# AV with stationary probabilities and a column of ones in V, rows scaled before a DMA transpose, in a chunk-attention and MLP kernel

## The chip, the cores and the metric

The kernel runs on one core of one Trainium2 chip. Its time is device microseconds of one execution. Engines that matter here: TensorE (PE, with its weight loads shown as PEld), VectorE (DVE), ScalarE (ACT), GpSimd (POOL) and SyncE (SP), which does no arithmetic and issues nearly all DMAs, in program order. The DMAs themselves run on 16 DMA engines that all queues share.

## The reference

Attention over chunks of 64 positions, 8 batches of 8 heads with 576 positions and 64 features, then an MLP with an exact GELU on the 4608 rows of 512 features:

```
scores = q_c @ k_c^T / sqrt(64)            # per head, per chunk of 64
attn   = exp(scores - max) / (sum + 1e-9)
x      = (attn @ v_c), heads side by side   # 4608 x 512
out    = gelu(x @ w_in) @ w_out             # 512 -> 2048 -> 512, f32 in, f32 out
```

The kernel works in bf16 with f32 sums, and leaves out the maximum (the scores are small).

## The kernel before

**Tiles.** The 4608 rows are nine tiles of 512 (`NT = 9`): tile t below 8 holds the first 512 positions of batch t, tile 8 the last 64 positions of all batches. A pass of the loop at L1003 does the MLP of tile t and, in the gaps, the attention of tile n = t+1. The result of the attention is `x`, kept transposed (features on partitions, `[128, 4, 512]`), because both operands of the first product need the contraction on partitions.

**The MLP of a tile.** `mm1_groups` (L582) does x @ w_in. It uses a seven-product scheme instead of eight block products for three of the four column groups (a, b, c) and plain products ("p") for the rest; the order is a string of words such as "begin 1a c1a p 6a 1b ...", read from left to right. The words 1 to 7 are the products, c and a are copies and additions on ACT and DVE, g the GELUs. Products 4 to 7 need sums of blocks of x, `x_sums` (L548, four DVE subtractions T1, T3, T2, T4). From tile 3 (`FIRST7`) on the second product is `mm2_seven` (L681), also seven products: X, Y(s2), X, Y(s1), Z(s3), Y(s4), Z, with hooks `also(0)` to `also(5)` between them. Tiles 0 to 2 use plain products in 16 slots of four matmuls (`mm2_slot`, L765).

**The attention of tile n.** `quad_S` (L224) does 64 small matmuls (64x64 blocks in the four quadrants of the array) into four PSUM banks, and four ACT exponentials make the probabilities `pT`, keys on partitions, queries along the free axis. Then, before the change:

- `quad_part` (L246), four times: a DVE transpose in 32x32 blocks and a DVE reduction give partial sums over keys.
- `quad_exchange` (L258) and `quad_across` (L271): small copies between partition groups, on ACT up to tile 3 and on POOL after it (`small`, L278).
- `quad_rb` (L264): totals and their reciprocals, DVE.
- `quad_rc` (L291), four times: a DVE transpose spreads the reciprocals along the partitions.
- `quad_av` (L296): 64 small matmuls with V stationary and `pT` moving; the result comes out transposed already.
- `quad_x` (L304), four times: a DVE multiplication of the PSUM result by the spread reciprocals writes `x`.

**Where these stand.** In pass 1 and 2 (`one_tile`, L990): S at slot 1, the partial sums at once, totals at slot 3, AV and `quad_x` and `x_sums` at slot 7; in pass 2 the S of tile 4 at slot 14. From pass 3 on: AV at `also(1)`, `x_sums` at `also(2)` and `also(3)`, the next S at `also(2)`, partial sums at `also(3)` to `also(5)`, and exchange, totals and the first spread in the words of the next `mm1_groups` (`totals_over_mm1`, L972; in pass 3 the words pt0 to pt3, ex0, ex1 of `FOURTH`).

**Loads.** All go through SP in program order: k and q of tile t+3, v of tile t+2 (`load_v_rows`, nine DMAs), 1 MB each, then the transposes of q and k by DMA (`flip`, L187, 16 blocks of 128x128 each, after POOL has cast them to bf16 at L160), and the stores of the output rows. Pass 3 and later issue them as `ahead` (L1027): flips of t+2, v of t+2, q and k of t+3. At most eight DMAs of SP are under way; a ninth waits for the first.

**PSUM.** Eight banks: `ps_mm` 3, `ps_tp` 2, `ps_at` 3. AV and S use two of `ps_tp` and two of `ps_at`.

Of the kernel before, what the change touches and what calls it, by code (L numbers as in the profile page):

```python
# [11 lines left out]
def kernel(  # L12
# [134 lines left out]
    def cast_v_plain(t, copy, ns=range(CT // 2)):  # L147
        st = tiles[t]
        if 0 in ns:
            st["v"] = ld.tile([P, H, CT // 2, D], bf16, tag="v", name="v_nat")  # L150
        for n in ns:
            copy(st["v"][:, :, n], st["vf"][:, :, n])
# [51 lines left out]
    def cast_v_rows(t, copy):  # L204
        st = tiles[t]
        st["v"] = ld.tile([P, H, CT // 2, D], bf16, tag="v", name="v_nat")
        for r in range(2):
            copy(st["v"][:, r::2], st["vf"][:, r::2])  # L208
# [32 lines left out]
    def quad_parts(t):  # L241
        for g2 in range(2):
            for c in range(2):
                quad_part(t, g2, c)

    def quad_part(t, g2, c):  # L246

        st = tiles[t]
        if c == 0:
            st["part", g2] = work.tile([P, 2, NB // 2, 2, 2], f32, tag="part", name="part", bufs=2)  # L250
        pt = work.tile([P, NB // 2, 32, 2], bf16, tag="pt", name="pt", bufs=2)
        nc.vector.transpose(
            pt[:].rearrange("p n e u -> p (n e u)").bitcast(f32).rearrange("p (n e) -> p n e", e=32),
            st["pT", 2 * g2 + c][:].rearrange("p i c -> p (i c)").bitcast(f32).rearrange("p (n e) -> p n e", e=32))
        nc.vector.tensor_reduce(st["part", g2][:, c, :, :, 0], pt[:].rearrange("p n e u -> p n u e"),  # L255
                                axis=mybir.AxisListType.X, op=mybir.AluOpType.add)

    def quad_exchange(t, g2):  # L258
        part = tiles[t]["part", g2]
        for s in range(G):  # L260
            o = s ^ 1
            small(t)(part[QD * s:QD * (s + 1), :, :, :, 1], part[QD * o:QD * (o + 1), :, :, :, 0])

    def quad_rb(t, g2):  # L264
        total, rb = (work.tile([P, 2, NB], f32, tag=nm, name=nm, bufs=2) for nm in ("total", "rb"))
        nc.vector.tensor_reduce(total[:], tiles[t]["part", g2][:].rearrange("p c n u s -> p c (n u) s"),
                                axis=mybir.AxisListType.X, op=mybir.AluOpType.add)
        nc.vector.reciprocal(rb[:], total[:])
        tiles[t]["rb0", g2] = rb

    def quad_across(t, g2):  # L271
        rb = tiles[t]["rb0", g2]
        across = work.tile([P, NB], f32, tag="across", name="across", bufs=2)
        tiles[t]["rb", g2] = rb[:, 0], across[:]
        for r in range(2):
            small(t)(across[CH * r:CH * (r + 1)], rb[CH * (1 - r):CH * (2 - r), 1])

    def small(t):  # L278
        return AC if t <= FIRST7 else PO

    def quad_total(t):
        for g2 in range(2):
            quad_exchange(t, g2)
        for g2 in range(2):
            quad_rb(t, g2)
            if g2 == 0:
                tiles[t]["rb", 0] = tiles[t]["rb0", 0][:, 0], None
                quad_rc(t, 0, 0)
            quad_across(t, g2)

    def quad_rc(t, g2, c):  # L291
        rc = work.tile([P, NB, 32], f32, tag="rc", name="rc", bufs=4)
        nc.vector.transpose(rc[:], tiles[t]["rb", g2][c].to_broadcast([P, NB, 32]))
        tiles[t]["rc", 2 * g2 + c] = rc

    def quad_av(t):  # L296
        st = tiles[t]
        st["av"] = four_banks("av_ps")
        for g2, u, g, n, r, c, o, rs, os in quadrants():
            nc.tensor.matmul(st["av"][g2][c][rs, u, :], st["v"][os, 2 * g + r, place(r, 2 * n + c)[1], :],  # L300
                             st["pT", 2 * g2 + c][os, u, :],
                             start=True, stop=True, tile_position=(CH * o, CH * r))

    def quad_x(t, g2, c):  # L304
        st = tiles[t]
        x = st["x"][:].rearrange("p g (n c e) -> p (g n) c e", c=2, e=CH)[:, CT * g2:CT * (g2 + 1), c]
        nc.vector.tensor_tensor(x.rearrange("p n (e u) -> p n e u", u=2),  # L307
                                st["av"][g2][c][:].rearrange("p n (e u) -> p n e u", u=2),
                                st["rc", 2 * g2 + c][:].rearrange("p (n u) e -> p n e u", u=2),
                                op=mybir.AluOpType.mult)  # L310
# [47 lines left out]
    def duo_av(t, g2):  # L358
        st = tiles[t]
        st.setdefault("av", {})[g2] = duo_banks(g2, "av_ps")  # L360
        for u, g, n, r, c, rs, cs in duos(g2):
            nc.tensor.matmul(st["av"][g2][c][rs, u, :], st["v"][cs, 2 * g + r, n, :], st["pT", 2 * g2 + r][cs, u, :],
                             start=True, stop=True, tile_position=(CH * c, CH * r))
# [39 lines left out]
    def att_rc(t, g):  # L403

        rb = tiles[t]["rb"]
        rc = work.tile([P, NB, 32], f32, tag="rc", name="rc", bufs=4)
        nc.vector.transpose(rc[:], rb[:, g].to_broadcast([P, NB, 32]))
        tiles[t]["rc", g] = rc
# [25 lines left out]
    def att_av(t, g2, ns):  # L434
# [5 lines left out]
        for g in (2 * g2, 2 * g2 + 1):  # L440
            for n, r, c, i, rs, cs in parity_blocks(ns):
                nc.tensor.matmul(st["av", g2][c][rs, g % 2, n], st["v"][cs, 2 * g + r, n, :], st["pT", g][cs, r, n],
                                 start=True, stop=True, tile_position=(CH * c, CH * r))
# [104 lines left out]
    def x_sums(t, which=(1, 3, 2, 4)):  # L548
# [7 lines left out]
        for i in which:  # L556
# [13 lines left out]
               g12c w2 w4 g21c"""  # L570

    FOURTH = """begin pt2 tab 1a 1b pt0 c1a c1b p 7a 6a 2a 2b 6b c2a pt3 5a g11a c3a c2b 1c 5b a1a c1c g11b 3a g22a
                pt1 6c c3b 4a 7b ex0 c2c a2a g12a ex1 2c g11c g21a p 3b a1b totals 4b a2b g12b 5c 7c c3c g22b a1c
                g21b p 3c 4c g22c h1 a2c g12c g21c rc0 h2 p h3"""
# [106 lines left out]
    def mm2_seven(t, at={}):  # L681
# [9 lines left out]
        X, Y, Z = (ps_mm.tile([P, 2, NH], f32, tag="mm", name="y_ps") for _ in range(3))  # L691
# [3 lines left out]
        if t == B:  # L695
            s1 = work.tile([P, 2, NH], f32, tag="y_1", name="y_1", bufs=1)
            last_seven(t, h, w, s, T, (X, Y, Z), (s1, s2, s5), y)
# [3 lines left out]
        AC(Y[:], X[:])  # L701
        h_third(t)
        also(1)
# [61 lines left out]
    def mm2_slot(t, ms, qt):  # L765
        st = tiles[t]
        if qt == 0:
# [101 lines left out]
    with tc.manual_schedule():  # L869
# [102 lines left out]
        def totals_over_mm1(n):  # L972

            at = ("begin", "totals", "rc0")
            units = [[lambda: quad_exchange(n, 0), lambda: quad_exchange(n, 1)],
                     [lambda: quad_rb(n, 0), lambda: quad_rb(n, 1), lambda: quad_across(n, 0),
                      lambda: quad_across(n, 1)],
                     [lambda: quad_rc(n, 0, 0)]]
            return dict(zip(at, units))
        def loads_at(t, nms="qk"):  # L980
            if t + 2 < NT:
                load_v_rows(t + 2)
            if t + 3 < NT:
                for nm in nms:
                    load_qk(t + 3, nm)
# [4 lines left out]
        def one_tile(n, more={}):  # L990

            at = {0: [lambda: act_table(Act.Exp)], 1: [lambda: quad_S(n), lambda: quad_parts(n)],
                  3: [lambda: quad_total(n)],
                  7: [lambda: quad_av(n), lambda: quad_x(n, 0, 0)]
                     + [u for m in range(1, G)
                        for u in (lambda m=m: quad_rc(n, m // 2, m % 2), lambda m=m: quad_x(n, m // 2, m % 2))]
                     + [lambda: x_sums(n)]}
# [5 lines left out]
        for t in range(1, NT):  # L1003
# [4 lines left out]
            if t == 1:  # L1008
# [5 lines left out]
                e1 = {"1a": [lambda: w_in_sums(slice(0, 2), "c")], "p": [lambda: load_v_rows(3)], "end": [lambda: w_sums((1, 3))]}  # L1014
                e2 = one_tile(2, {5: [lambda: act_table(Act.Gelu)],
                                  8: [lambda: flips_of(3), lambda: loads_of_qk(4)]})
            elif t == 2:
# [3 lines left out]
                e1.update({f"w{i}": [lambda i=i: w_sums((i,))] for i in (2, 4)})  # L1021
                flips_of(4)
                loads_at(2, "q")
                cast_v_rows(4, PO)
                e2 = one_tile(3, {8: [lambda: load_qk(5, "k")], 14: [lambda: quad_S(4)]})
            elif n < NT:
                def ahead(t=t):  # L1027
                    if t + 2 < NT:
                        flips_of(t + 2)
                    loads_at(t)  # L1030
                e1 = totals_over_mm1(n)
                if t == FIRST7:
                    pool_cast_q(t + 2)
                    del e1["begin"]
                    e1["tab"] = [lambda: act_table(Act.Gelu)]
                    e1.update({f"ex{i}": [lambda i=i: quad_exchange(n, i)] for i in range(2)})
                    e1["totals"] += [lambda: pool_cast_k(FIRST7 + 2), ahead]
                    e1.update({f"pt{i}": [lambda i=i: quad_part(n, i // 2, i % 2)] for i in range(G)})
                else:
                    if t + 2 < NT:  # L1040
# [45 lines left out]
```

## Time and profile before

| | us |
|---|---|
| runs | 273.24, 275.71, 277.56 (median 275.71) |
| profiled execution | 274.82 |
| its span | 273.0 |
| outside the span | 1.8 |
| PE busy | 260.3 (95%) |
| DVE busy | 220.4 (81%) |
| ACT busy | 181.8 (67%) |
| POOL busy | 91.2 (33%) |

The span is the time from the first to the last instruction of the program; the granted TensorE clock was 1.0. Groups of instructions are given as line, engine, operation, output<-input, shape, and a count, then busy us and the mean ns of one. Where two instructions of an engine follow each other without a pause, the next starts a little before the first ends, so that sums of means are up to a tenth too high. "SPq" rows are the issuing time on SP, not the transfer; the time from issue to landing is a separate figure. The passes are seen in the trace by the first X product of each: pass 2 begins at 80.75, pass 3 at 109.50, pass 4 at 136.99, pass 5 at 163.92, pass 6 at 190.84, pass 7 at about 217.6, pass 8 at about 243.5 us.

Landing times, from issue to landing (median): q loads of 1 MB 6.2 us, k loads of 256 KB 6.2 us, v loads of 128 KB 3.0 us, stores of 256 KB 3.3 us, transposes of q 4.9 us and of k 3.8 us.

### The profile page before, as it was taken

Reading aid. Unit: us, or ns where it says so; the run is one execution under the profiler, and the core shown is the slowest. Engines: PE = TensorE matmul, PEld = TensorE weight load, DVE = VectorE, ACT = ScalarE, POOL = GpSimd, SP = SyncE. Lnnn points to the kernel's source line nnn. Section 1 sums busy time; section 2 is a strip of 40 time slices with the busy share of each in tenths; the row PEclk is TensorE's granted clock in tenths of the full one; section 3 lists DMA queues with packets and bytes.
Section 4 is the critical chain, followed back from the end, with each engine's and each line's share of the span. In section 5 each row is a group of like instructions: output and inputs, shape, how many; then the busy total and the mean of one; then the engine's idle time right before and its main releaser. Section 6 shows DMA issues by size and latency. Waiting matters only on the chain.

```text
span 273.0 us, 7454 instructions
## 1 busy us (share of the span) xinstructions
PE 260.3 (95%) x2984; PEld 187.3 (69%) x3009; DVE 220.4 (81%) x386; ACT 181.8 (67%) x353; POOL 91.2 (33%) x180
## 2 busy tenths in 40 slices
PE   8689999999999999999999999999999999999993
PEld 2454454486448644768887888788878887888782
DVE  2663586979796999999989998999899889945852
ACT  3557755788667966986679567946884787338700
POOL 2725667360460443370372355133510321000000
PEclk9999999999999999999999999999999999999999
DMA  6999999996999998999899796987983410130005
GB/s 202 258 359 405 396 394 246 242 268 151 347 222 241 279 176 181 273 231 188 231 265 248 219 249 93 237 192 155 251 121 86 143 41 2 38 111 7 4 0 154
DMA packets 118066, 53.96 MB, mean 198 GB/s; under 512 B 93456, under 2 KB 112912, under 8 KB 118032
## 3 DMA queue, kind: packets, MB, share of 16 engines
q1 hardware_dynamic: 117712, 52.97, 74.8%
q8 instruction: 23, 0.38, 0.6%
q10 hardware_dynamic: 320, 0.52, 0.5%
q14 instruction: 11, 0.09, 0.1%
HBM read 36.70 MB, written 9.44 MB: 169 GB/s over the span
## 4 chain that ended last, share of the span: by engine, by line
PE 80%; DVE 7%; SPq 4%; ACT 3%; DMA 3%; issue 1%; POOL 0%; ACTq 0%; DVEq 0%
PE y_ps L673 27%; PE h_Y L611 11%; PE h_ps L631 8%; PE h_Z L611 8%; PE h_X L611 8%; PE y_ps L771 6%; PE h_ps L481 5%; PE y_ps L795 4%; DMA arrival<-in_moe_w_in_dram 3%; SPq L145 2%; PE s_ps L230 1%; SPq L112 1%; DVE part L255 1%; DVE x L368 1%; ACT y_ps L701 1%
## 5 line engine op out<-in xcount | busy, mean ns | idle before, releaser
L611 PEld LDWEIGHTS <-w_in_s 128*128 128x128 bf16 x384 | 37.4, 98 | 6.8
L673 PEld LDWEIGHTS <-h_s 128*128 128x128 bf16 x384 | 37.0, 98 | 5.4 <-DVE h_s L513 0.8
L673 PE MATMUL y_ps<-w_t,h_s 128*128 128x256 bf16 x288 | 34.7, 273 | 0.3
L611 PEld LDWEIGHTS <-w_in_sb 128*128 128x128 bf16 x288 | 28.1, 98 | 8.3 <-issue 2.0
L208 POOL CAST v_nat<-arrival 128x1024 bf16<-128x1024 f32 x14 | 15.4, 1106 | 53.3 <-DMA arrival<-in_v_dram 46.7
L160 POOL CAST q_nat<-arrival 128x512 bf16<-128x512 f32 x33 | 22.2, 711 | 32.5 <-DMA arrival<-in_q_dram 24.2
L771 PE MATMUL y_ps<-w_out_sb,h 128*128 128x512 bf16 x137 | 31.5, 379 | 1.3 <-issue 1.0
L673 PEld LDWEIGHTS <-h 128*128 128x128 bf16 x288 | 28.2, 98 | 4.7
L631 PE MATMUL h_ps<-x,w_in_sb 128*128 128x512 bf16 x103 | 27.8, 379 | 0.7
L611 PE MATMUL h_Y<-x_t,w_in_s 128*128 128x256 bf16 x192 | 27.6, 272 | 0.0
L611 PE MATMUL h_X<-x,w_in_sb 128*128 128x256 bf16 x192 | 26.8, 273 | 0.0
L655 DVE TENSOR_TENSOR y<-h_Z,y 128x512 f32<-128x512 f32 x32 | 21.6, 680 | 5.8 <-PE h_Z L611 4.9
L160 POOL CAST k_nat<-arrival 128x512 bf16<-128x512 f32 x34 | 22.1, 684 | 11.6 <-DMA arrival<-in_k_dram 7.6
L771 PEld LDWEIGHTS <-h 128*128 128x128 bf16 x144 | 13.4, 98 | 15.6 <-issue 0.8
L673 PE MATMUL y_ps<-w_out_sb,h 128*128 128x256 bf16 x192 | 22.9, 273 | 0.0
L618 ACT ACTIVATE h<-y 128x512 bf16<-128x512 f32 x32 | 20.1, 628 | 1.7 <-DVE y L655 1.6
L867 ACT ACT_TABLE_LOAD x16 | 20.5, 1283 | 1.0 <-PEq L1070 0.7
L644 ACT COPY h_Y<-h_X 128x512 f32<-128x512 f32 x24 | 14.0, 584 | 10.5 <-PE h_X L611 10.4
L255 DVE TENSOR_REDUCE part<-pt 128x16 f32<-128x512 bf16 x28 | 19.2, 686 | 1.0
L633 ACT ACTIVATE h<-h_ps 128x512 bf16<-128x512 f32 x29 | 17.1, 595 | 2.6 <-PE h_ps L631 1.2
L307 DVE TENSOR_TENSOR x<-av_ps,rc 128x512 bf16<-128x512 f32 x28 | 18.0, 670 | 0.6
L631 PEld LDWEIGHTS <-w_in_sb 128*128 128x128 bf16 x116 | 11.4, 98 | 7.7
(129 smaller groups left out, 488.7 us busy)
## 6 DMA issues: line engine op xcount, KB each, us to landing
out_dram<-y_sb SPq DMA_DIRECT2D x32, 256.0 KB, 3.3
arrival<-in_q_dram SPq DMA_DIRECT2D x7, 1024.0 KB, 6.2
arrival<-in_k_dram SPq DMA_DIRECT2D x24, 256.0 KB, 6.2
arrival<-in_v_dram SPq DMA_DIRECT2D x42, 128.0 KB, 3.0
arrival<-in_moe_w_out_dram SPq DMA_DIRECT2D x4, 1024.0 KB, 12.4
arrival<-in_v_dram SPq DMA_DIRECT2D x8, 256.0 KB, 8.3
arrival<-in_moe_w_in_dram SPq DMA_DIRECT2D x4, 512.0 KB, 7.3
arrival<-in_moe_w_in_dram SPq DMA_DIRECT2D x2, 1024.0 KB, 10.4
```

The lines of the kernel that those rows point to most:

```text
L160: copy(st[nm][:, g].rearrange("p j r d -> p r j d"), st[nm + "f"][:, 2 * g:2 * g + 2])
L208: copy(st["v"][:, r::2], st["vf"][:, r::2])
L255: nc.vector.tensor_reduce(st["part", g2][:, c, :, :, 0], pt[:].rearrange("p n e u -> p n u e"), axis=mybir.AxisListType.X, op=mybir.AluOpT ...
L307: nc.vector.tensor_tensor(x.rearrange("p n (e u) -> p n e u", u=2), st["av"][g2][c][:].rearrange("p n (e u) -> p n e u", u=2), st["rc", 2 ...
L611: nc.tensor.matmul(banks[g + name][:, i], lhs[:, kk, i], rhs[:, kk], start=fresh and i == kk == 0, stop=(kk == 1), skip_group_check=True)
L618: nc.scalar.activation(h[:, j:j + 2, m], src[:], Act.Gelu)
L631: nc.tensor.matmul(bank[:], w_in_sb[:, ks, f * P:(f + 1) * P], st["x"][:, ks, :], start=(ks == 0), stop=(ks == KS - 1))
L633: nc.scalar.activation(st["h"][:, f, :], bank[:], Act.Gelu)
L655: TT(sums[g, i][:], banks[g + "Z"][:], sums[g, i][:], op=add)
L673: nc.tensor.matmul(out[m], lhs[:, f, m * P:(m + 1) * P], rhs[:, f, :], start=fresh and f == 0 and (m == 0 or len(out) == 3), stop=(f == FH ...
L771: nc.tensor.matmul(y_ps[:], st["h"][:, f, ms * P:(ms + 1) * P], w_out_sb[:, f, :], start=(f == 0), stop=(f == FF - 1))
L867: nc.scalar.activation(act_scratch[:], rest[:, 0:1], func)
```

## The change

- V gets a 65th column (`D + 1`), set to ones by a small POOL memset from tile 2 on (`FIRSTX = 2`; "the third tile").
- `quad_part`, `quad_exchange`, `quad_rb`, `quad_across`, `quad_total`, `quad_rc` and `quad_x` are gone. `rows_av` has `pT` stationary and V moving: 64 matmuls with 65 columns each, into six banks of seven (or two) blocks of 65: two of `ps_tp`, three of `ps_at`, one of `ps_mm`. Queries now lie on partitions, and column 64 is the sum of each row.
- `rows_x` takes, bank by bank, a reciprocal of the sums and a multiplication into `x_r` (bf16, SBUF), and transposes `x_r` into `x` with two DMAs on SP, 7 blocks after the second bank, 9 after the sixth.
- The `ps_mm` bank is that of the fourth row block (pass 1 and 2) or the Z bank of `mm2_seven`, whose allocation moves behind the first copy; `h_third` moves behind `also(1)`.
- AV stands at slot 6 instead of 7 and `x_sums` at slot 14 (pass 1 and 2), or at `also(4)`. Two of the `w_sums` (2 and 4) move from pass 2 to pass 1, behind `rows_x`.
- Loads: v of tile 3 and 4 move behind the transposes of x of passes 1 and 2; in pass 3 and later `ahead` issues v of t+2, the flips and q of t+3, and `behind` at `also(2)` issues k of t+3 (and v of tile 8). In pass 3 the flips come before v.

```diff
+            nc.gpsimd.memset(st["v"][:, :, :, D:], 1.0)
...
+    def rows_av(t, last):
+        banks = [pool.tile([P, MT], f32, tag=tag, name="av_ps")
+                 for pool, tag in ((ps_tp, "tp"),) * 2 + ((ps_at, "at"),) * 3] + [last]
+        st["av"] = [b[:, :NX * (D + 1)].rearrange("p (i e) -> p i e", e=D + 1) for b in banks]
+        for b in range(G * CT // 2):
             for c in range(2):
...
+                for r in range(2):
+                    bank, i = 2 * (b // NX) + r, b % NX
+                    g, n, o = b // (CT // 2), b % (CT // 2), c ^ r
+                    os, cs = slice(CH * o, CH * (o + 1)), slice(CH * c, CH * (c + 1))
+                    nc.tensor.matmul(st["av"][bank][cs, i, :],
+                                     st["pT", 2 * (g // 2) + c][os, CT // 2 * (g % 2) + n, :],
+                                     st["v"][os, 2 * g + r, place(r, 2 * n + c)[1], :],
+                                     start=True, stop=True, tile_position=(CH * o, CH * c))
+    def rows_x(t):
+        rows = work.tile([P, G * CT // 2, 2, D], bf16, tag="x_r", name="x_r", bufs=1)
+        xT = st["x"][:].rearrange("p g (n e) -> p (g n) e", e=P)
+        def flip_rows(b0, b1):
+            nc.sync.dma_start_transpose(xT[:, b0:b1], rows[:, b0:b1].rearrange("p b r d -> p (b r d)"))
+        for bank in range(6):
+            b0 = NX * (bank // 2)
+            ni = min(NX, G * CT // 2 - b0)
+            av = st["av"][bank][:, :ni]
+            one = work.tile([P, NX], f32, tag="one", name="one", bufs=2)
+            nc.vector.reciprocal(one[:, :ni], av[:, :, D])
+            to = rows[:, b0:b0 + ni, bank % 2]
+            nc.vector.tensor_tensor(to, av[:, :, :D], one[:, :ni].to_broadcast([P, ni, D]), op=mybir.AluOpType.mult)
+            if bank == 1:
+                flip_rows(0, NX)
+        flip_rows(NX, G * CT // 2)
...
-                  3: [lambda: quad_total(n)],
-                  7: [lambda: quad_av(n), lambda: quad_x(n, 0, 0)]
...
+            at = {0: [lambda: act_table(Act.Exp)], 1: [lambda: quad_S(n)],
+                  6: [lambda: rows_av(n, bank_of_rows()), lambda: rows_x(n)], 14: [lambda: x_sums(n)]}
...
+                                  6: [lambda: w_sums((2, 4))], 7: [lambda: load_v_rows(3)], 8: [lambda: flips_of(3), lambda: loads_of_qk(4)]})
...
+                load_qk(5, "q")
+                e2 = one_tile(3, {7: [lambda: load_qk(5, "k")], 8: [lambda: load_v_rows(4)], 14: [lambda: quad_S(4)]})
...
                 def ahead(t=t):
+                    if t > FIRST7 and t + 2 < B:
+                        load_v_rows(t + 2)
                     if t + 2 < NT:
                         flips_of(t + 2)
-                    loads_at(t)
+                    if t == FIRST7:
+                        load_v_rows(t + 2)
+                    load_ahead(t, "q")
+
+                def behind(t=t):
+                    if t + 2 == B:
+                        load_v_rows(B)
+                    load_ahead(t, "k")
...
+                    e1["begin"] = [lambda: pool_cast_qk(5), lambda: cast_v_rows(4, PO), ahead]
...
+                e2 = {1: [lambda: rows_av(n, tiles[n - 1]["Z"]), lambda: rows_x(n)], 2: [behind], 3: [], 4: [lambda: x_sums(n)]}
```

More of the change, by code (lines that the diff above doesn't have):

```diff
@@ L258, in quad_exchange @@
[L258 to L310, printed above, removed]
+    NX = MT // (D + 1)
@@ L405, in att_rc @@
         rb = tiles[t]["rb"]
[L406 removed]
+        rc = work.tile([P, NB, 32], f32, tag="rc", name="rc", bufs=2)
         nc.vector.transpose(rc[:], rb[:, g].to_broadcast([P, NB, 32]))
@@ L690, in mm2_seven, with bank_mm @@
         T = [None] + [w_t[i] for i in range(1, 5)]
-        X, Y, Z = (ps_mm.tile([P, 2, NH], f32, tag="mm", name="y_ps") for _ in range(3))
+        def bank_mm():
+            return ps_mm.tile([P, 2, NH], f32, tag="mm", name="y_ps")
+        X, Y = bank_mm(), bank_mm()
         s2, s5 = (work.tile([P, 2, NH], f32, tag=nm, name=nm, bufs=1) for nm in ("y_2", "y_5"))
@@ L766, in mm2_slot @@
         st = tiles[t]
-        if qt == 0:
+        if qt == 0 and ("y_ps", ms) not in st:
             st["y_ps", ms] = ps_mm.tile([P, d_model], f32, tag="mm", name="y_ps")
@@ L1037 @@
[L1037 to L1040, printed above, removed]
-                        e1["begin"] += [lambda: pool_cast_k(t + 2)]
-                    e1["begin"] += [ahead]
-                e2 = {1: [lambda: quad_av(n), lambda: quad_rc(n, 0, 1), lambda: quad_x(n, 0, 0), lambda: quad_x(n, 0, 1),
-                          lambda: quad_rc(n, 1, 0), lambda: quad_rc(n, 1, 1),
-                          lambda: quad_x(n, 1, 0), lambda: quad_x(n, 1, 1)],
-                      2: [lambda: x_sums(n, (1, 3))], 3: [lambda: x_sums(n, (2, 4))]}
+                e2 = {1: [lambda: rows_av(n, tiles[n - 1]["Z"]), lambda: rows_x(n)], 2: [behind], 3: [], 4: [lambda: x_sums(n)]}
```

81 lines of the change are left out of this document (27 added, 54 removed).

## The prediction

> **What bounds the kernel.** I read the page's busy shares and chain first.
>
> ```profile
> PE 260.3 (95%) x2984; PEld 187.3 (69%) x3009; DVE 220.4 (81%) x386; ACT 181.8 (67%) x353; POOL 91.2 (33%) x180
> ...
> DMA  6999999996999998999899796987983410130005
> ...
> PE 80%; DVE 7%; SPq 4%; ACT 3%; DMA 3%; issue 1%; POOL 0%; ACTq 0%; DVEq 0%
> ```
>
> PE carries the chain, and the DMA engines are full until slice 31 (some 210 us). Next the stretches by pass (length; busy PE, PEld, DVE, ACT, POOL; clock, DMA share, GB/s):
>
> ```profile
> 53.33:80.75 27.42, 26.76 (x285) 16.66 (x288) 23.01 (x41) 20.57 (x45) 10.97 (x16) 1.00 0.93 246
> 80.75:109.50 28.75, 28.17 (x353) 17.60 (x357) 25.67 (x44) 21.58 (x47) 9.38 (x11) 1.00 1.02 220
> 109.50:136.99 27.49, 27.16 (x342) 21.79 (x341) 26.81 (x48) 21.27 (x38) 9.82 (x23) 1.00 0.96 230
> 136.99:163.92 26.93, 26.78 (x340) 21.82 (x341) 25.45 (x44) 19.55 (x35) 12.75 (x26) 1.00 0.96 245
> 163.92:190.84 26.92, 26.77 (x340) 21.89 (x341) 25.04 (x44) 19.55 (x35) 9.88 (x22) 1.00 0.85 169
> ```
>
> PE idles 0.66, 0.58, 0.33, 0.15 and 0.15 us in them, and 0.15 each in passes 6 and 7: 2.2 us in all. The rest of its 12.7 idle us lies before 53 and in the last pass, which the change does not touch. DVE is nearly as full, but what it ends late costs PE at most those 2.2 us.
>
> **What is removed and added**, by shape:
>
> ```profile
> L255 DVE TENSOR_REDUCE part<-pt 128x16 f32<-128x512 bf16 x28 | 19.2, 686 | 1.0
> L307 DVE TENSOR_TENSOR x<-av_ps,rc 128x512 bf16<-128x512 f32 x28 | 18.0, 670 | 0.6
> L252 DVE STREAM_TRANSPOSE pt<-pT 128x256 f32<-128x256 f32 x28 | 12.2, 436 | 2.0 <-ACT pT L237 2.0
> ...
> L450 DVE TENSOR_TENSOR x<-av_ps,rcs 128x256 bf16<-128x256 f32 x4 | 1.5, 420 | 0.9 <-PE av_ps L442 0.9
> ...
> L421 DVE RECIPROCAL rr<-sT 128x8 f32<-128x8 f32 x2 | 0.4, 208 | 0.8 <-PE sT L416 0.8
> ```
>
> DVE loses per tile four each of these transposes, reductions and multiplications (0.436 + 0.686 + 0.670), four spreads (0.697), two totals (0.190), two reciprocals (0.353): 11.0 us. It gains six reciprocals (0.208, L421) and six multiplications; 670 ns for 512 and 420 for 256 elements make 0.98 ns an element, so 0.607 for 448 and 0.294 for 128: 1.25 + 2.43 + 0.59 = 4.3 us. Seven tiles save 47 us of DVE, 5.1 of ACT (16 x 219 + 8 x 202 ns), 12.2 of POOL (40 x 209 + 20 x 193 ns; seven memsets of about 0.13 come in, L63). All of it lies beside PE: worth 0 to 2.2 us, and I take 1.0, nearest to passes 1 and 3, whose DVE queues it empties. POOL's casts of V now write runs of 65: 1.1 us (L208) to double that, under POOL's two thirds idle.
>
> AV stays 64 small matmuls. It takes 0.67 us in the chain, and so does S, which visits the quadrants in another order; in the trace four start within 12 ns and the next four 32 ns later. A 65th column adds 27/64 ns to each group of four: nothing. If the new order of quadrants ran them one by one, 64 x 27 ns (a quarter of the 109 ns pitch of a 256-column matmul) would be 1.75 us, 7.5 in seven tiles. I take nothing, the row of S and AV being nearer.
>
> **A pass from the fourth on.** T0 is the end of AV (152.23 in pass 4); the next pass starts at T0+11.5, and its first product that needs `x_sums` (6a, third of four subtractions, 1.8 us) at T0+12.8. So the second transpose has to land by T0+10.9. DVE ends its h sums at 152.99, T0+0.8; bank 2 is done at T0+2.4, bank 6 at T0+5.0. Sixteen blocks land 3.8 (k) to 4.9 us (q) after issue, so nine land by T0+9.9 at the full price: hidden with 1 us to spare, 3 at half of it. `h_third` now follows the six banks: 5.0 + 1.22 gives T0+6.2, just when Z needs it (158.41, T0+6.2): 0 to 0.1 us a pass, 0.5 in five; I take 0.2.
>
> **SP, where the transposes have to pass.** What stands ahead of them in pass 2 and 3:
>
> ```profile
> 94.41 2.15 SPq L193 DMA_TRANSPOSE q_t<-q_nat  x1
> 98.80 1.61 SPq L193 DMA_TRANSPOSE k_t<-k_nat  x1
> 100.46 5.30 SPq L126 DMA_DIRECT2D arrival<-in_v_dram  x9
> 105.80 0.60 SPq L112 DMA_DIRECT2D arrival<-in_q_dram  x1
> 106.50 1.00 SPq L787 DMA_DIRECT2D out_dram<-y_sb  x2
> 107.55 8.45 SPq L106 DMA_DIRECT2D arrival<-in_k_dram  x4
> ...
> 124.78 5.98 SPq L126 DMA_DIRECT2D arrival<-in_v_dram  x9
> 130.80 0.60 SPq L112 DMA_DIRECT2D arrival<-in_q_dram  x1
> ```
>
> SP never rests here, and a transfer waits for those ahead: the store issued at 67.23, behind two loads of 1 MB, landed after 8.1 us, not 3.3; the q load of 130.80 landed at 136.62. A pair of q and k transposes between two landings took 3.9 us (144.38 to 148.17), so the 16 blocks of x cost 2.0 to 2.4 of this full stream.
>
> Pass 1: AV at slot 6 ends at 71.7, bank 6 at 75.5; the loads ahead have landed by 75.4, so x lands at 78.8, 1.5 us before pass 2 needs it. v of tile 3 follows only then: SP is 3 us later at the flips of tile 3 (k_u lands at 87.9; DVE reaches `in_order` at 89.3, covering it by 1.4), and k of tile 4 lands at 97.0, not 95.4.
>
> Pass 2: POOL casts k of tile 4 (3.34 us) before SP can go on, so its flip goes out at 100.4 and lands at about 104.1, 2.9 before S at 107.0 needs it; q of tile 5 at 102.0, landing at 108.2 (4.2 us of stream, as 132.43 to 136.62); a store; then x of tile 3, ready on DVE since 103.5, lands at 111.2. Pass 3 would start at 109.2 and needs T3 for 7a, its fourth step: 112.5 instead of 111.2. Late by 1.3 us (0 to 3).
>
> Pass 3: x of tile 4 stands behind k and v of tile 4/5, both flips, v and q of tile 6. From k of tile 4 (95.4) to q of tile 6 (136.6) the same set took 41.2 us before, 3.7 of them gaps. Now it starts at 97.0 and has x of tile 3 in it (2.2): 97.0 + 41.2 + 2.2 = 140.4, or 136.7 without the gaps. x lands 2.2 later, 138.9 to 142.6, and T2 1.85 after that; 6a ran at 138.14 before. Late by 2.6 to 6.3, the delay of pass 2 included; DVE, which stands in `x_sums` meanwhile, holds back a store and the next copies, and these hold nothing else. I take 4.0, near the middle: pass 3 showed gaps before (POOL's copies of L262 and L276) that are gone, and has no new ones but for the casts of tile 5. v of tile 4 (cast by 122.4) is still 3 us before its AV; past that each us would be paid.
>
> Pass 4 and later: v, flips, q, k, x and stores need about 23.5 us of stream in 26.9, so the lag melts and the first reckoning holds.
>
> Sum: 274.8 (the profiled execution, 0.9 below the median) - 1.0 + 0.2 + 4.0 = 278.0; with one half of the 0.9 added, since the runs scatter from 273.2 to 277.6, **278.5 us**.
>
> **Rivals.** The bound of 2% is 5.5 us, about what a measurement of this kernel can tell from no change: 269.3 and 280.3 around 274.8.
>
> - *The full stream decides more* (chance 0.23): the gaps stay and each x pair costs what q_t cost at 117.48 (3.98 us of issue). Two of these in place of 2.2 add 3.5 to 142.6, and a half of it less: late by 8 to 10, 282 to 284. For it: SP's 3.98; against: k_t's 1.6 to 2.2. From a lag of 5.5 us on it is over the bound.
> - *Nothing is held* (0.18): SP reaches x in time, and it lands after 3.8 to 4.9 us everywhere. Then PE's 2.2 idle us are all that is left: 272.6 to 274.8, say 273.9. Against it: the store of 67.23.
> - *AV one quadrant after another* (0.03): 278 + 7.5, 285.5.
> - *A gain over 2%* (0.03): only if PE's own matmuls ran closer together; no idle time in the passes supports it.
> - *Each block pays by itself* (0.01): nine blocks have 5.9 us (T0+5.0 to T0+10.9), so it decides from 0.65 us a block on; at twice that the 16 blocks run 20.8 us from bank 2, to T0+23.2, 12.3 late in seven passes: 361. Against it: 16 blocks land in 3.8 to 4.9, 0.24 to 0.31 each.
>
> The Trainium skill (VectorE: DVE Perf Modes, "The three transpose paths") prices a 128x128 bf16 transpose by DMA at 1309 ns and by TensorE at 390, which is that last rival and speaks against this change. The trace disagrees for many blocks in one DMA (0.24 us each at best), and the measurement decides.
>
> The forecast has the remaining 0.52; its own range is 277.0 to 280.8 (late by 2.6 to 6.3), of which I put 0.04 over the bound. So faster 0.03; within 2% 0.48 + 0.18 = 0.66; slower 0.04 + 0.23 + 0.03 + 0.01 = 0.31. The range, 273.5 to 283.5, leaves out the gain (0.03), the two dear rivals (0.04), the top of the stream's case (0.06) and the bottom of the unheld one (0.05).
>
> **What would show it.** Right: DVE about 175 us busy, PE unchanged in busy time, S and AV at 0.67; PE idle 1 to 2 us at the start of pass 3 and 2 to 5 at that of pass 4, released by DVE's `x_sums` or the transposes of x, which wait on SP behind the q loads; none in passes 5 to 8. Wrong: x landing under 5 us after bank 6 in pass 3; PE waiting in every pass (then on `h_third` or the Z bank); AV above 1 us.

## The result and the profile after

| | before | after |
|---|---|---|
| runs, us | 273.24 to 277.56 (4), median 275.5 | 283.48 to 287.22 (4), median 285.25 |
| profiled execution (span) | 274.82 (273.0) | 284.48 (282.7) |
| PE busy | 260.3 | 265.5 |
| DVE busy | 220.4 | 173.0 |

The changed kernel is slower: the ratio is 1.038, with an interval from 1.027 to 1.049. Said were 278.5 us and a range up to 283.5; the time lies above the range. The page of the changed kernel first (busy us and share; then the granted clock and the DMA engines in 40 slices; then the chain's shares):

```profile
PE 265.5 (94%) x3009; PEld 188.8 (67%) x3009; DVE 173.0 (61%) x330; ACT 176.9 (63%) x329; POOL 78.8 (28%) x127
...
PEclk9599999999999999999979999999999999999998
DMA  7999998997989999998999979999943642151004
...
PE 69%; DVE 12%; DMA 11%; SPq 3%; ACT 2%; issue 2%; POOL 1%; DVEq 0%; ACTq 0%; POOLq 0%
```

DVE lost 47 us, as reckoned, and the chain grew longer all the same: DMA's share in it went from 3% to 11%. In slice 21 the clock digit is 7: PE ran at half clock for part of it, which no slice of the kernel before shows. (The 5 in slice 2 lies in the first 15 us, before the passes that the change touches; the last section comes back to it.) The stretches by pass (columns as in the prediction):

```profile
53.89:81.08 27.19, 27.17 (x286) 16.64 (x286) 22.40 (x38) 18.16 (x33) 10.40 (x16) 1.00 0.94 240
81.08:111.73 30.65, 29.23 (x357) 17.63 (x356) 13.19 (x26) 18.94 (x35) 8.93 (x13) 1.00 1.11 239
111.73:141.71 29.98, 27.29 (x341) 21.75 (x341) 17.51 (x35) 21.19 (x37) 8.96 (x14) 1.00 0.94 222
141.71:171.88 30.17, 28.57 (x340) 22.44 (x341) 19.44 (x39) 19.82 (x35) 10.33 (x14) 0.94 1.00 230
171.88:198.80 26.92, 26.90 (x345) 22.12 (x343) 17.64 (x36) 19.56 (x35) 6.85 (x11) 1.00 1.01 211
```

Against 28.75, 27.49, 26.93 and 26.92 before, pass 2 is 1.9 us longer, pass 3 2.5, pass 4 3.2, pass 5 not at all; 0.3 were lost ahead of pass 2 and 1.7 behind pass 5. That is the whole 9.7 us. PE's gaps in them, from the trace: 1.25 us in pass 2 (93.00 to 94.25, waiting for DVE, which waits at `in_order` for k_u); 0.17 + 1.24 at the start of pass 3 and 1.37 + 1.58 at that of pass 4, all released by the transposes of x; and 1.66 in pass 7 (233.85 to 235.51), released by ACT's copy `h_sb` of group c. The longest waits of PE (who waited for what; us in total, times, longest), and then that copy of ACT, which had itself waited for a store:

```profile
PE h_ps L602 <- DMA x<-x_r: 2.8, 2, 1.6
PE h_Y L582 <- ACT h_sb L623: 1.7, 1, 1.7
PE h_X L582 <- DMA x<-x_r: 1.5, 2, 1.4
PE h_Z L582 <- DVE h_sb L626: 1.3, 1, 1.3
```

```profile
234.87 0.58 ACT L623 COPY h_sb<-h_Y 128x512 f32<-128x512 f32 x1 [2.20 <-DMA out_dram<-y_sb]
```

In pass 4 there is one thing more: from 144.38 on the clock is at half for 3.41 us, in which eight matmuls of 256 columns took 1.85 us (at 146.14) and the next eight at full clock 1.04, so about 1.7 us, half of it, are lost with PE busy (28.57 against 26.78).

This is where x waits, on SP (start, issuing time, operation):

```profile
103.30 0.57 SPq L112 DMA_DIRECT2D arrival<-in_q_dram  x1
103.97 0.53 SPq L762 DMA_DIRECT2D out_dram<-y_sb  x1
104.59 6.03 SPq L270 DMA_TRANSPOSE x<-x_r  x2
...
134.76 0.61 SPq L112 DMA_DIRECT2D arrival<-in_q_dram  x1
135.47 5.01 SPq L270 DMA_TRANSPOSE x<-x_r  x2
```

A pair of transposes behind a q load of 1 MB holds SP for 5 to 6 us; in passes 4 to 7 one transpose takes 1.2 to 1.6. The second of each pair landed 7.19 us (114.19) and 6.89 us (144.07) after its issue.

### The profile page after: what moved, and what is told of

It reads as the page before. It is cut to its first block, busy times and chain, and to the rows that moved or that the text cites. A ratio compares the mean times of both kernels' runs of the same rounds, so it can differ in the third digit from the quotient of the medians.

```text
span 282.7 us, 7352 instructions
## 1 busy us (share of the span) xinstructions
PE 265.5 (94%) x3009; PEld 188.8 (67%) x3009; DVE 173.0 (61%) x330; ACT 176.9 (63%) x329; POOL 78.8 (28%) x127
## 4 chain that ended last, share of the span: by engine, by line
PE 69%; DVE 12%; DMA 11%; SPq 3%; ACT 2%; issue 2%; POOL 1%; DVEq 0%; ACTq 0%; POOLq 0%
PE y_ps L644 22%; PE h_Y L582 9%; PE h_Z L582 7%; PE h_X L582 6%; PE h_ps L602 6%; DMA x<-x_r 5%; PE h_ps L452 4%; PE y_ps L746 4%; PE y_ps L770 4%; DVE x_r L278 2%; DVE h_s L484 2%; DMA k_u<-k_nat 2%; DMA arrival<-in_k_dram 2%; DVE h_s L483 2%; SPq L126 2%
## 5 line engine op out<-in xcount | busy, mean ns | idle before, releaser
L602 PE MATMUL h_ps<-x,w_in_sb 128*128 128x512 bf16 x116 | 30.3, 383 | 2.8 <-DMA x<-x_r 2.8
L746 PE MATMUL y_ps<-w_out_sb,h 128*128 128x512 bf16 x144 | 32.8, 380 | 0.0
L160 POOL CAST k_nat<-arrival 128x512 bf16<-128x512 f32 x34 | 20.6, 642 | 33.9 <-DMA arrival<-in_k_dram 24.8
L582 PE MATMUL h_X<-x,w_in_sb 128*128 128x256 bf16 x192 | 27.7, 279 | 1.5 <-DMA x<-x_r 1.5
L623 DVE COPY y<-h_Y 128x512 f32<-128x512 f32 x16 | 11.0, 686 | 20.8 <-PE h_Y L582 19.4
L278 DVE TENSOR_TENSOR x_r<-av_ps,one 128x448 bf16<-128x448 f32 (+1 forms) x35 | 19.5, 558 | 1.2
```

Of the source, the lines that this page charges most:

```text
L160: copy(st[nm][:, g].rearrange("p j r d -> p r j d"), st[nm + "f"][:, 2 * g:2 * g + 2])
L278: nc.vector.tensor_tensor(to, av[:, :, :D], one[:, :ni].to_broadcast([P, ni, D]), op=mybir.AluOpType.mult)
L582: nc.tensor.matmul(banks[g + name][:, i], lhs[:, kk, i], rhs[:, kk], start=fresh and i == kk == 0, stop=(kk == 1), skip_group_check=True)
L602: nc.tensor.matmul(bank[:], w_in_sb[:, ks, f * P:(f + 1) * P], st["x"][:, ks, :], start=(ks == 0), stop=(ks == KS - 1))
L746: nc.tensor.matmul(y_ps[:], st["h"][:, f, ms * P:(ms + 1) * P], w_out_sb[:, f, :], start=(f == 0), stop=(f == FF - 1))
```

## Experiments

The theory after the result: AV, DVE and the new chain cost nothing; the loss is the transposes of x standing on SP among loads, and it is paid wherever the next reader of the late queue is: x itself, k_u, the stores. The clock adds to it. Each kernel was timed together with the kernel before on the same chip (median 274.2 to 275.0 there).

**1. Without the transposes of x.** `rows_x` writes its rows straight into x.

```diff
-        rows = work.tile([P, G * CT // 2, 2, D], bf16, tag="x_r", ...)
+        rows = st["x"][:].rearrange("p g (n r d) -> p (g n) r d", r=2, d=D)
-                flip_rows(0, NX)
-        flip_rows(NX, G * CT // 2)
```

> The transposes of x by DMA are left out: the rows go untransposed into x, so the output is not the reference's; all loads, the six banks, the scaling on DVE and the moved sums stay. Theory (the loss is x landing late behind loads on SP, and the clock at half after the stalls): the gaps of PE at the starts of pass 3 and 4 (0.17 + 1.24 + 1.37 + 1.58 us) are gone, the granted clock stays at 1.0 from pass 2 to 7 (1.7 us back), and the gap before in_order's product (1.25) shrinks, since SP reaches the flips of tile 3 some 3 us sooner; the gap of 1.66 us in pass 7 stays. About 277.5 to 279 us, a ratio of 1.01 to the kernel before. Rival (the 65-column AV, the new DVE chain or the order of the loads cost it): 283 to 286, no different from the changed kernel. Rival (the clock falls whatever PE waits for): a half-clock period between 100 and 270 us in spite of the missing gaps.

274.99 us, a ratio of 1.001 (0.997 to 1.004): less than the theory had given. Busy times and granted clock of its page:

```profile
PE 260.7 (96%) x3009; PEld 187.2 (69%) x3009; DVE 173.3 (64%) x330; ACT 176.4 (65%) x329; POOL 80.3 (30%) x127
...
PEclk9999999999999999999999999999999999999999
```

No gap over 0.2 us is left in passes 2 to 4, the gap of pass 7 is 0.17 instead of 1.66, and the clock stays at full. So all of the loss hangs on the transposes, the one in pass 7 too. The same run says what the rest of the change is worth together, DVE's relief of 47 us among it: nothing that can be measured.

**2. The transposes issued, and nobody waits for them.** As in 1, but the two DMAs are issued, from x into a dead buffer.

```diff
+        rows = st["x"][:].rearrange("p g (n r d) -> p (g n) r d", r=2, d=D)
+        xT = work.tile([P, G * CT // 2, P], bf16, tag="x_r", name="x_dead", bufs=1)
```

> The rows go untransposed into x, as in the run without transposes (so the output is not the reference's), but the two transposes of x are issued all the same, from x into a buffer that nobody reads. So SP and the stream carry them, and nothing waits for their landing. Theory (two parts: x itself late, about 6 us with the clock; and what the transposes push back on SP, about 3 us): the gaps at the starts of pass 3 and 4 and the half clock are gone, those in pass 2 (some 1.2) and pass 7 (some 1.6) stay: 275.0 + 2.9 = 278. Rival (only the wait for x costs): 275 to 276, no gap in passes 2 and 7. Rival (it is the load on the stream itself, through other loads that land late): 281 or more.

285.43 us (1.039, 1.031 to 1.047), as slow as the changed kernel; this is over what the theory gave, and its rival of 281 or more has the time. The gaps that the theory left in passes 2 and 7 are there (1.30 and 1.75 us). But there is a third, which it did not have, and what PE waits for there is not a load: it stands from 145.72 to 151.03, 5.31 us, for one copy of ACT. SP and ACT there:

```profile
133.47 0.61 SPq L112 DMA_DIRECT2D arrival<-in_q_dram  x1
134.18 5.89 SPq L270 DMA_TRANSPOSE x_dead<-x  x2
140.16 0.53 SPq L737 DMA_DIRECT2D out_dram<-y_sb  x1
140.75 4.17 SPq L106 DMA_DIRECT2D arrival<-in_k_dram  x4
145.02 2.22 SPq L737 DMA_DIRECT2D out_dram<-y_sb  x3
```

```profile
150.39 0.59 ACT L623 COPY h_sb<-h_Y 128x512 f32<-128x512 f32 x1 [5.86 <-DMA arrival<-in_v_dram]
```

`h_sb` of group c takes a buffer of the output rows (`ypool`, two of them), so it may be written when the stores of pass 3 have left it. These stand on SP behind the dead transposes and four k loads, and the one that empties the first of the two buffers lands at 150.24, 0.15 ahead of the copy. The label names a load of v, but none landed between 135.6 and 151.0, and the semaphore that ACT waited for until then is that of this store, issued at 146.25. Without anyone waiting for x, PE runs ahead into the same hole in SP's queue, 5 us later. Two windows of half clock follow (148.09 to 154.92). So the held queue costs PE time also where nobody waits for x; in the changed kernel x was only the first of its readers.

**3. q behind x.** The q loads of tiles 5 and 6 are moved behind the transposes of x.

```diff
-                load_qk(5, "q")
-                e2 = one_tile(3, {7: [lambda: load_qk(5, "k")], ...
+                e2 = one_tile(3, {7: [lambda: loads_of_qk(5)], ...
...
-                    load_ahead(t, "q")
+                    if t > FIRST7:
+                        load_ahead(t, "q")
...
+                    if t == FIRST7:
+                        load_ahead(t, "q")
                     load_ahead(t, "k")
+                    if t == FIRST7:
+                        pool_cast_q(t + 3)
...
```

> The changed kernel with the q loads of tiles 5 and 6 moved behind the transposes of x (in pass 2 into slot 7 with k; in pass 3 to also(2), with POOL's cast of it). Theory: x of tile 3 and 4 land 3.5 to 4.5 us sooner, the time of one load of 1 MB on the full stream: before 110.5 and before 140.5, so the gaps at the starts of pass 3 and 4 are gone and with them the half clock: 4.4 + 1.7 us less, about 279 us. Rival (the two transposes take 7 us under any load, for the reads of the stream that are still there): gaps of 1 us and more stay at both places, 283 or more.

279.52 us (1.018, 1.010 to 1.025), 5.7 us less, of 6.1 expected. x of tile 3 lands at 104.45 and 106.66, 3.0 and 3.3 us after issue; x of tile 4 at 134.68 and 136.02. The load ahead was the price, and the half clock is gone with the gaps. 0.68 us of gap is left at `in_order`, and the stores of pass 3 now stand behind five loads, so that the copy `h_sb` is late in pass 4: a new gap of 2.12 us (145.05 to 147.17), and 1.04 in pass 7.

**4. v of tile 8 first.** The 16 loads that stood ahead of the stores of pass 6 are issued at the start of that pass.

```diff
-                    if t == FIRST7:
+                    if t == FIRST7 or t + 2 == B:
                         load_v_rows(t + 2)
...
-                    if t + 2 == B:
-                        load_v_rows(B)
```

> The changed kernel with the 16 loads of v of tile 8 moved from also(2) of pass 6 to its start, behind the flips of tile 8. Theory (three stores of pass 6 stand on SP behind these loads, ACT's copy into the same buffer waits for them, and PE for ACT): the gap of 1.66 us in pass 7 is gone, about 1.7 us less, 283.5. Rival (the copy waits for something else): the gap stays at 1.3 us or more and the time at 285. A rival in place: x of tile 7 now stands behind these loads and a new gap of 1 us or more opens at the start of pass 7.

284.02 us (1.036, 1.028 to 1.044), which these runs cannot tell from the changed kernel. The gap at `h_sb` is gone, and the rival in place came true: 1.23 us at the start of pass 7 for x of tile 7, which now stands behind those loads.

**5. The flips of tile 3 ahead of v of tile 3.**

```diff
-   7: [lambda: load_v_rows(3)], 8: [lambda: flips_of(3), lambda: loads_of_qk(4)]
+   7: [lambda: flips_of(3)], 8: [lambda: load_v_rows(3), lambda: loads_of_qk(4)]
```

> The changed kernel with the flips of tile 3 ahead of the nine loads of v of tile 3 on SP (slots 7 and 8 of pass 1 exchanged). Theory: k_u lands at 86 to 88 instead of 91.7, so in_order no longer waits and the gap of 1.25 us in pass 2 is gone. Whether it shows in the time is open: if x of tile 3 lands when the stream lets it, pass 3 begins no sooner and the gap there grows from 1.4 to 2.6 us (time 285); if everything is shifted, 284. Rival (DVE itself is late at in_order): the gap of 1.25 stays.

282.86 us (1.029, 1.021 to 1.036). k_u lands at 86.89 and the gap in pass 2 is gone; in its profiled run x of tile 3 was late instead (4.30 us at the start of pass 3). That run had a half clock through most of its first 25 us, so only where the gaps are is read from it, and whether the time gained is not settled: the interval overlaps that of the changed kernel.

**6. The sums of group c in buffers of their own.**

```diff
-                    pair = ypool.tile([P, 4, TH], f32, tag="y", name="h_sb")
-                    sums[g, 0], sums[g, 1] = pair[:, 0:2], pair[:, 2:4]
+                    for m in range(2):
+                        sums[g, m] = work.tile([P, 2, TH], f32, tag="rc", name="h_sb", bufs=2)
```

> The changed kernel with only the two sums of group c in buffers of their own. Theory (ACT's copy h_sb waits for three stores that SP issues behind v of tile 8): the gap of 1.66 us in pass 7 is gone with nothing new in its place, and the stalls of passes 2, 3 and 4 stay: about 1.7 us less, 283.5. Rival (the copy waits for something else): the gap stays.

286.30 us in two runs. No gap is left from 151 us on, so the cause named for pass 7 is right. The time is not lower: in this run the earlier gaps were 2.57 (pass 2), 4.51 (pass 3) and 1.15 + 2.52 (pass 4), 10.8 us against 5.6 in the profile after. So SP was held several us longer here than in the profile after, with the DMAs in the same order. There is one profile of each, so whether the new buffers did it or it varies from run to run is not shown.

**7. All three moves** (3, 5 and 6).

> Three moves together on the changed kernel: q of tiles 5 and 6 behind the transposes of x, the flips of tile 3 ahead of v of tile 3, and the two sums of group c (h_sb) in buffers of their own instead of the buffers of the output rows. Theory: of the gaps that the order of q alone left (0.68 at in_order, 2.12 and 1.04 at ACT's copy h_sb in pass 4 and 7, which stood behind stores on SP) none over 0.5 us is left in passes 2 to 8, the clock stays at 1.0 there, and the time is 279.5 - 3.8 = 275.7, no more than 1% from the kernel before. Rival (the stream is full and a gap closed at one place opens at the next): gaps of 2 us or more in sum and 277.5 or more.

279.51 us (1.018, 1.013 to 1.023). The theory fell here and its rival held: the gaps at `in_order` and `h_sb` are closed, and gaps of 3.9 us in all (those over 0.15 us) stand elsewhere, 3.2 of it at the starts of pass 4, 5 and 6, where x of tiles 4 to 6 is late. In pass 4 a q load (156.99) is again right ahead of x (157.67; landed at 166.22, 8.55 us).

**8. q behind x in every pass** (7, and `load_ahead(t, "q")` always in `behind`).

> All on SP as in the run of the three moves, but with q behind the transposes of x in every pass from the second on. Theory (the gaps of 1.0 to 1.6 us that the three moves left at the starts of pass 4, 5 and 6 are x behind q of tile 7 and 8 again): those of passes 5 and 6 are gone, 1.6 to 2.6 us less: 277 to 278. Rival (a full stream: what is relieved in one place is late in the next): the gaps move to k, S or the stores and the time stays at 279.5.

278.99 us (1.012, 1.003 to 1.020). The gaps of passes 5 and 6 are gone; 1.45 + 0.39 are left at the start of pass 4, with a half-clock window behind them. The median hardly moved, within what these runs can tell.

**9. And v of tile 5 behind x** (8, and its loads and cast moved to also(2) of pass 3).

```diff
-                    if t == FIRST7:
-                        load_v_rows(t + 2)
...
-                    if t + 2 == B:
-                        load_v_rows(B)
+                    if t == FIRST7 or t + 2 == B:
+                        load_v_rows(t + 2)
+                    if t == FIRST7:
+                        cast_v_rows(t + 2, PO)
...
```

> The run with q late in every pass, and besides the nine loads of v of tile 5 (and POOL's cast of it) moved from the start of pass 3 to also(2), behind the transposes of x and ahead of q and k. Theory (all of the loss is what SP issues ahead of x, and no transfer is left there now): x of tile 4 lands 3 us sooner, at 136 to 138.5, the gaps of 1.45 and 0.39 us at the start of pass 4 and the half clock behind them are gone: 2 to 3.5 us less, 275.5 to 277, no more than 1% from the kernel before. Rival (a full stream): v of tile 5, q and k now land so late that AV, POOL's casts or S of passes 4 and 5 wait: 279 or more. No version of it is expected under 274, since the run without transposes was 275.0.

276.53 us in twelve runs, a ratio of 1.006 (1.003 to 1.009). SP where x of tile 4 is issued, and the time to landing of the transposes of x (the trace has it for twelve of the fourteen):

```profile
129.63 3.62 SPq L270 DMA_TRANSPOSE x<-x_r  x2
133.35 0.55 SPq L737 DMA_DIRECT2D out_dram<-y_sb  x1
133.96 5.83 SPq L126 DMA_DIRECT2D arrival<-in_v_dram  x9
139.83 0.61 SPq L112 DMA_DIRECT2D arrival<-in_q_dram  x1
```

```profile
DMA to landing us min/median/max: 2.9/3.4/3.7
```

None of these takes more than 3.7 us any more, and no gap of PE is released by x. So the order on SP is nearly the whole loss: the same DMAs, issued in another order, with `h_sb` in buffers of its own (which alone did not lower the time, experiment 6), cost 0.6% instead of 3.8%. What is left are gaps of 1.34 (S waiting for the flip of k of tile 6) and 0.54 + 0.63 (`h_sums`, DVE's sums for the second product).

**10. The transposes issued by ACT** instead of SP, behind ACT's copies of the two products after AV.

```diff
-            nc.sync.dma_start_transpose(xT[:, b0:b1], ...)
+            nc.scalar.dma_start_transpose(xT[:, b0:b1], ...)
...
         AC(y[0][:, :, :NH], X[:])
+        tiles[t + 1]["flip_rows"][0]()
...
         AC(s5[:], Y[:])
+        tiles[t + 1]["flip_rows"][1]()
...
```

> The changed kernel with the two transposes of x issued by ACT instead of SP, behind ACT's copies of the first and the second product after AV (slots 9 and 12 in passes 1 and 2); nothing else moves. Theory (the loss is the order on SP: there each transpose of x stood 3.3 to 4.5 us behind a load, with all that follows it): x lands 3 to 5 us after issue, SP runs as in the run without transposes, the gaps at the starts of pass 3 and 4 and in pass 7 are gone with the half clock: 275 to 277.5. Rival (the transposes' share of the full stream is the loss, wherever they are issued): x still lands 7 us after issue at passes 3 and 4, or q, k and v land later and PE waits for them: 280 or more. Rival (ACT is held by the issuing, 1.3 to 4 us each, and its copies are late for PE): gaps of 1 us and more released by ACT in every pass, 280 or more.

287.43 us (1.044, 1.037 to 1.051): the cure failed, and the time is that of both rivals. ACT in pass 2:

```profile
105.84 0.59 ACT L757 COPY y_sb<-y_ps 128x512 f32<-128x512 f32 x1 [2.92 <-PE y_ps L746]
109.32 2.21 ACTq L270 DMA_TRANSPOSE x<-x_r  x1
111.63 2.07 ACT L239 ACTIVATE pT<-s_ps 128x512 bf16<-128x512 f32 x4 [5.21 <-PE h_X L580]
```

x_r was complete at 104.14, but the transpose went out at 109.32, and behind it wait the exponentials of tile 4, whose PSUM banks PE needs next: a gap of 1.91 us, released by `pT`. What ACT waited for at 109.27 is in the trace: a semaphore on which a k load that SP had issued at 101.74 landed at 109.25, and on which the transpose then lands itself. The eight landing semaphores are shared by both queues, so ACT's transposes wait for SP's loads too. The transposes of x took 4.2 to 8.3 us to land, no less than on SP (2.9 to 7.2). This has the sign of the first rival; of the second there is this one gap and not one in every pass, so how the loss divides between the two is open.

**11. The same, with the flips of tile 3 first.**

> The same, and the flips of tile 3 ahead of v of tile 3 on SP. Theory: whatever gap at in_order is left (SP is 3 us earlier there, but so it was when nobody read x, and 1.3 us of gap stayed) is gone: up to 1.2 us less than with ACT's transposes alone, 274.5 to 276.5. Rival: no difference, since the gap is gone already.

289.4 to 297.0 us in four runs, far over the theory's 274.5 to 276.5. In pass 1 the transposes of SP (q_t, k_u) and of ACT (x) now meet, and each starts where the one before has landed: q_t lands at 76.20 and x goes out at 76.38; x lands at 79.39, k_u goes out at 79.53; k_u lands at 83.16, the second of x goes out at 83.25 and lands at 88.13, and PE has waited 7.9 us. The Trainium skill (DMA: Bandwidth & Descriptors, "Silent corruption: two transposing streams in flight at once") says that transposes issued from SP and from ACT must be serialized by a wait for the landing; the order in this trace agrees with that, with 0.1 to 0.2 us between a landing and the next issue. On one queue they overlap: in the profile after q_t of tile 6 goes out at 153.06, k_t at 154.95, and q_t lands at 157.23.

**12. An idle PE and the clock.** The kernel of 1, with 22 dead additions on DVE ahead of `x_sums` of tile 6.

```diff
-  4: [lambda: x_sums(n)]}
+  4: [lambda: [nc.vector.tensor_tensor(hold[:], rest[:], rest[:], op=add) for _ in range(22 if n == 6 else 0)],
+      lambda: x_sums(n)]}
```

> The run without transposes of x (output not the reference's) with 22 dead additions on DVE ahead of x_sums of tile 6 in pass 5, so that PE waits once, at the start of pass 6, for about 6 us. Theory (the granted clock is set window by window, in windows of 3.41 us that run from the start: a window with over 2 us of idle PE is followed by one at half clock): one or two half-clock windows of 3.41 us right after this gap, and none else from pass 2 to 7; the time grows by more than the gap itself, by 1.7 us a window. Rival (the clock falls for reasons of its own): no such period near pass 6.

The granted clock on its page, in 40 slices:

```profile
PEclk9999999999999999999999999996599999999999
```

The gap came out at 8.19 us (191.02 to 199.21), more than the 6 expected, and three windows at half clock lie on it, from 193.67 to 203.91, where the clock had been full in the run without the additions. The span is 282.8 against 272.1, one run of each: 10.7 us more, 2.5 over the gap, which is near half of the 4.7 us from the gap's end to the clock's return (2.35).

## Why the prediction failed, point by point

*What was right.* DVE at 173.0 (about 175 said); AV at 0.76 us from its first start to its last end in six of seven passes (0.74 before; 0.99 in the first), so the order of quadrants costs nothing; the multiplication of 448 elements took 0.62 (0.607 said), the reciprocal 0.20; `h_third` is not waited for; seven or nine blocks land together in 3.0 to 3.3 us where no load is ahead (experiment 3), so no block pays by itself; passes 5 and 6 hide the transposes, as reckoned by T0. The place was right too: SP, at the starts of pass 3 and 4. The idle times of PE that x would release there, 1 to 2 and 2 to 5 us, came as 1.41 and 2.95. Experiment 1 settles that the rest of the change, taken together, costs no time.

*The step that failed: when x lands on SP's queue at the starts of pass 3 and 4.* The sum's largest term, 4.0 us, was the delay of the product 6a in pass 4 (2.6 to 6.3), with 1.3 of it (0 to 3) at 7a in pass 3. 7a ran at 115.11 where it had run at 111.08, 4.0 late; 6a at 145.32 where it had run at 138.14, 7.2 late, above the top of its range. Both follow the landing of x: at 114.19, where 111.2 was said, with 7a 0.9 behind it; and at 144.07, where the 4.0 stands for 140.3 (138.14 + 4.0 - 1.85) and 142.6 was the latest, with 6a 1.25 behind it. That the idle time of PE released by x, 1.41 + 2.95 = 4.36 us, is close to the 4.0 is luck: part of the delay had already been spent at `in_order`.

*The price of a pair on SP*, in that landing, was put at 2.0 to 2.4 us of stream, from two flips whose landings were 3.8 us apart (144.38 and 148.17; the prediction has 3.9). From the landing ahead (a store at 110.81, q of tile 6 at 140.74) to that of the second transpose it was 3.4 and 3.3 us, and the pairs held SP for 6.03 and 5.01 us. The pair is 1.1 of the 3.0 us at pass 3; the other 1.9 are q of tile 5, which landed at 110.09 instead of 108.2. At pass 4 it is 1.1 of the 3.8, and q of tile 6 the rest. The 3.98 us of one q_t in the trace of before was seen and given to the rival of the full stream, at 0.23; as a price per pair it was nearer to what came than the one taken, and so was its time of 282 to 284. Experiment 3 shows that the load ahead makes the difference: with the q load behind, the same pair takes 2.6 us of issue, and each transpose lands 3.0 to 3.3 after issue. Why a pair is dearer behind such a load was not tried.

*The cover of 1.4 us at `in_order`* was not there. k_u was put at 87.9, but the prediction's own 3 us of lag on SP, added to its landing in the trace of before (86.60), makes 89.6, later than the 89.3 at which DVE needs it. It landed at 91.73: its flip went out 3.8 us later than before (86.44 instead of 82.66), behind v of tile 3, and took 5.29 us instead of 3.95. This is the gap of 1.25 us. Experiment 5 closes it, and in its profile the wait for x at the start of pass 3 was longer instead, so I count it as a part of the 7.2 and not as a price of its own; the times of that experiment do not settle this.

*The stores were left out.* The prediction asked when loads and x land, not when stores do. ACT's copy `h_sb` shares their buffers, so SP's lag was paid in pass 7 (1.66) as well, where no waiting of PE had been said (experiments 2, 4 and 6).

*The clock was left out* of every term: 1.7 us in the profile after, half of the 3.41 us from 144.38 on, and 1.2 of it behind 6a (experiment 12, and the count of windows below).

*DVE's relief* was taken at -1.0 us. Experiment 1 gives 0.0 (-0.3% to +0.4%) for it and the rest of the change together: some small gaps of the kernel before vanish, and nothing that can be measured comes of it.

With these in place the sum comes out: 278.5, and 3.2 for the delay at 6a, 1.2 for the half clock behind it, 1.7 for the stores, 1.0 for the gain that did not come, less the 0.2 of `h_third`, makes 285.4; measured were 285.25. The range ended at 283.5 because none of its cases had a term for the stores or the clock. All of these hang on one thing, that SP is held by the transposes: without them (experiment 1) all are gone.

*What stays open.* Why the same order of DMAs was held 5 us longer in one profile than in another (experiment 6 against the profile after) was not tried. No version beat the kernel before: the best is 9, 0.6% behind it, and 1, which leaves the transposes out, is at 1.001.

## What to carry to other kernels

A DMA put on an in-order queue is priced by what stands ahead of it on that queue, and it charges every later reader of that queue, stores included: list them all, for taking one reader away (experiment 2) only moves the wait to the next. When an engine is relieved that is not on the path, as DVE here, expect nothing from it, and ask first whether the replacement's transfers can be put ahead of the large prefetches. Moving them to another queue was no cure here: transposes waited for each other's landing across the two queues (experiment 11), and for loads with which they share landing semaphores (experiment 10).

## What the hardware showed that was not expected

**The clock falls by windows.** The changes of the granted clock lie on a grid of 3.41 us in every trace (4.44, 7.85, 14.68, 144.38, 147.80 after). I counted PE's idle time in each window of that grid behind 53 us, in the traces of before, after and all twelve runs but for the last pass. Of 17 windows with 1.85 us or more of idle time, 16 were followed by a window at half clock (the other had 2.00); of those with 1.66 or less none was, unless the clock was already at half. So two gaps of 1.37 and 1.58 us cost a window when 2.32 us of them fell into the same one, and gaps of 1.25, 1.66 and, split over two windows, 2.12 us cost none. The Trainium skill (TensorE: Matmul & The Clock Gate, "Part 1: The HAM clock gate") states a free-running window of 3413 ns and half clock after an idle window; the length agrees with these traces, but a window with 1.85 of its 3.41 us idle was enough here (experiment 8).

**The start varies too.** Half-clock windows at 7 to 25 us appear in some profiled runs and not in others: none in those of before, 1 and 3; two after; four in that of 9 (7.60 to 21.25). The instructions of the first 25 us are the same in all of them; what makes the difference is not shown.
